# A fused attention and two feed-forward layers on one core: the stores of the weight and x2 jobs move from the SyncE queue to the ScalarE queue

## The chip, the core and the metric

The kernel runs on one core of one Trainium2 chip. The metric is the device time of one execution in microseconds (us), taken outside the profiler as the median of several runs. A profile is one more execution, recorded instruction by instruction.

## What is computed

Attention over short windows, then two feed-forward layers, in float32. The reference, cut to what matters:

```python
for c in range(S // 32):                      # B, H, S, D = 4, 8, 768, 64
    k_full = cat(mem_k, k[:, :, 32*c-16 : 32*c+40])   # 8 + 56 keys, clipped at the ends
    a = softmax(q_c @ k_full.T / 8)
    out_c = a @ cat(mem_v, v[same window])
x = out.reshape(3072, 512)
h = x @ w_in            # 512 x 2048
x = softplus(h) @ w_out # 2048 x 512, first layer
h = x @ w_in2
y = (h - tanh(h)) @ w_out2   # second layer
```

## The kernel before, in words

Each float32 operand of a matmul is split into a high part and a low part, and three products (high·high, high·low, low·high) make one product. The splits cost ScalarE a copy and VectorE a subtraction each, and both are needed for weights (`w`), inputs (`x`) and activations (`gh`, `gl`).

The 3072 tokens are worked in this order. Up to about 427 us, the first layer goes over tiles of 512 tokens in the plain way (`ff_h`, `ff_y1`), while the attention units that are still to come run between its matmuls. From there, four phases of 1024 tokens (the last third of layer 1, then all of layer 2) use a Strassen-like scheme with 7 products in place of 8: `h_phase` (about 76 us) and then `y_phase` (about 76 us) for each. In `h_phase` a product takes TensorE 1.36 us and goes to one of eight accumulator banks. ScalarE copies the partial results out (`kept`, line 701), VectorE adds (`sum`, line 706), and ScalarE applies softplus or tanh (lines 427 and 737).

The scheme needs weights and inputs that are sums of blocks. *Jobs* prepare them beside the main work: `job_w1` and `job_w` (weights of layers 1 and 2) and `job_x` (inputs of a phase). A job reads a tile, forms the sums on VectorE, splits them into high and low parts in buffers of the pool `o` (four buffers; `job_x` also uses `gh` and `gl`), and stores those to scratch memory in DRAM: `wid` (w_in), `wod` (w_out), `x2d` (inputs). `Ring.add` (line 684) and `x2_load` (line 645) load them again later. `job_w` begins with the load of a raw weight tile (line 477, named `w<-in_w2i` or `w<-in_w2o`), and `LEAD` = 3 ticks later it uses it on ScalarE (line 481). Lines 463 and 467 split into `o`; line 600 does the high part in `job_x`.

The order is fixed by hand. A *tick* (function `tick`) is one step of the schedule: it first issues what was deferred to this tick, then the instructions of the main chain, and then one step of each active job. Every engine executes its instructions in the order in which the program emits them. The DMAs are all issued by SyncE (SP in the profile), which does nothing else, so a transfer that has to wait for its data holds up every transfer behind it:

```python
lo = opool.tile([P, *shape], F32R, name="o")
nc.vector.tensor_tensor(out=lo, in0=src, in1=hi.bitcast(F32), op=ALU.subtract)
defer(put, lo, dst(1))          # line 468: issued at the start of the next tick
```

The compiled program tells of a DMA's landing by one of eight semaphores, DMAHW0 to DMAHW7. All DMAs of the program take them in turn, in program order, whichever engine issues them. Before a DMA is issued, its engine waits until the DMA that had the same semaphore before it (eight places earlier) has landed, unless the engine is known to have waited for that already.

Of the kernel before, what the change touches and what calls it, by code (L numbers as in the profile page):

```python
# [8 lines left out]
F32 = mybir.dt.float32  # L9
# [90 lines left out]
def attention_ffn_ffn(  # L100
# [10 lines left out]
    nc = tc.nc  # L111
# [105 lines left out]
    def run(steps):  # L217
        for _ in steps:
            pass
# [4 lines left out]
    def x_tile(j):  # L224
        if j not in xt:
            xt[j] = xpool.tile([P, KT, 2, N], F32R, name=f"x{j % 2}")
        return xt[j]
# [3 lines left out]
    def qk_load(u):  # L231
        t = apool.tile([P, NPAIR * (P + NCH * KEYS)], F32, name="qk")
        nc.sync.dma_start(out=t, in_=qk[u])
        q = t[:, : NPAIR * P].rearrange("p (a t) -> p a t", a=NPAIR)
        k = t[:, NPAIR * P :].rearrange("p (c a k) -> p c a k", c=NCH, a=NPAIR)
        att[u] = dict(q=q, k=k)
# [18 lines left out]
    def v_load(u, v=None):  # L255
        v = apool.tile([P, NCH, NPAIR, D], F32, name="v") if v is None else v
        nc.sync.dma_start(out=v.rearrange("p c a d -> p (c a d)"), in_=vv[u])
        att[u]["v"] = v
# [76 lines left out]
    def t_mm(u, ps):  # L335
        a = att[u]
        for p in range(NPAIR):
            nc.tensor.transpose(  # L338
                ps[:, p * P : (p + 1) * P], a["sm"][:, p * P : (p + 1) * P], ident
            )  # L340
        a["t"] = ps

    def t_out(u):
        a = att[u]
        if u < UB:
            pT = early[:, UB + u].rearrange("p (a t) -> p a t", a=NPAIR)
        else:
            pT = apool.tile([P, NPAIR, P], F32, name="pT", bufs=1)
        a["pT"] = pT
        nc.scalar.copy(out=pT.rearrange("p a t -> p (a t)"), in_=a.pop("t"))  # L350
# [110 lines left out]
    def split_to(src, dst, shape):  # L461
        hi = opool.tile([P, *shape], F32R, name="o")
        nc.scalar.copy(out=hi, in_=src)
        yield
        put(hi, dst(0))
        lo = opool.tile([P, *shape], F32R, name="o")
        nc.vector.tensor_tensor(out=lo, in0=src, in1=hi.bitcast(F32), op=ALU.subtract)
        defer(put, lo, dst(1))

    def put(t, places):  # L470
        for at, n, place in places:
            nc.sync.dma_start(out=place, in_=t[:, at : at + n].bitcast(F32))

    def job_w(kind, p, slot):
        src = w2i if kind == "i" else w2o
# [107 lines left out]
    def job_x(b, e, slot, spare):  # L583
        raw = wpool.tile([P, 2, 2, N], F32, name=f"w{slot}")
        nc.sync.dma_start(out=raw, in_=y1d[b][e])
        for _ in range(LEAD):
            yield
        b11, b21, b12, b22 = raw[:, 0, 0], raw[:, 0, 1], raw[:, 1, 0], raw[:, 1, 1]
        o = {}

        def high(q, src):
            if spare and q in (2, 5, 7):
                h, l = (gpool.tile([P, N], F32R, name=n) for n in ("gh", "gl"))
                stores = [(x2d[b][q - 1][:, e, s], t) for s, t in enumerate((h, l))]
            else:
                t = opool.tile([P, 2, N], F32R, name="o")
                h, l = t[:, 0], t[:, 1]
                stores = [(x2d[b][q - 1][:, e], t)]
            o[q] = h, l, src, stores
            nc.scalar.copy(out=h, in_=src)  # L600

        def low(q):
            h, l, src, stores = o.pop(q)
            minus(l, src, h.bitcast(F32))
            for place, t in stores:
                defer(nc.sync.dma_start, place, t.bitcast(F32))

        high(1, b11)
        high(2, b21)
        yield  # L610
        low(1)
        low(2)
        minus(b12, b12, b11)
        high(3, b22)
        yield
        low(3)
        minus(b22, b22, b12)
        high(5, b12)
        yield
        low(5)  # L620
        minus(b11, b22, b11)
        high(6, b22)
        yield
        low(6)
        minus(b21, b21, b22)
        high(7, b11)
        yield
        low(7)
        high(4, b21)
        yield  # L630
        low(4)
# [77 lines left out]
    def minus(out, x, y):  # L709
        nc.vector.tensor_tensor(out=out, in0=x, in1=y, op=ALU.subtract)  # L710
# [126 lines left out]
        if f == NF - 1:  # L837
            out1(j)

    plan, now, active, late = {}, [0], [], []  # L840
    W2 = [("i", p) for p in range(NP)] + [("o", p) for p in range(NP)]
    for t, kind, p in JOBS_W1:
        plan.setdefault(t, []).append(lambda x=(kind, p): job_w1(*x))
# [7 lines left out]
    place = [0, 0]  # L851
    soft = {}

    def defer(f, *args, more=0):
        late.append((now[0] + more, f, args))

    def tick(chain=iter(())):
        k = now[0]
        now[0] += 1
        calls, late[:] = [x for x in late if x[0] <= k], [x for x in late if x[0] > k]  # L860
        for _, f, args in calls:
            f(*args)
        if k in starts:
            place[:] = starts[k], k
        i, r = place[0], k - place[1]
        u = ATT_ORDER[i] if i < len(ATT_ORDER) else None
        before = ATT_ORDER[i - 1] if 0 < i <= len(ATT_ORDER) else None
        if u is not None:
            if r == 1:
                if i + 2 < len(ATT_ORDER):  # L870
                    qk_load(ATT_ORDER[i + 2])
                if 0 < i < len(ATT_ORDER) - 1:
                    v_load(ATT_ORDER[i + 1])
                next(soft[u])
            elif r == 2:
                run(soft.pop(u))
        if r == 1 and before in VIA_DRAM:
            run(soft.pop(("x", before)))
        if r == 0 and before is not None:
            v_mm(before, ps_a)  # L880
        if r == 0 and u is not None:
            s_mm(u, ps_a)
        if r == 4 and u is not None:
            t_mm(u, ps_a[:, 0, :])
        next(chain, None)
        if r == 4 and u is not None:
            t_out(u)
        next(chain, None)
        if r == 0 and before is not None:
            soft["x", before] = (x_out if before // UB < PLAIN else x_out_whole)(before)  # L890
            next(soft["x", before])
        if r == 0 and u is not None:
            soft[u] = softmax(u)
            next(soft[u])
        if r == 0 and before is not None:
            next(soft["x", before], None)
        run(chain)
        active.extend(job() for job in plan.get(k, ()))
        for job in active[:]:
            if next(job, active) is active:  # L900
                active.remove(job)

    with tc.manual_schedule(engines={mybir.EngineType.PE}):
# [10 lines left out]
        if True:  # L914
# [31 lines left out]
            for token in OPENING.split():  # L946
# [7 lines left out]
                elif op == "Z":  # L954
                    for _ in range(i):
                        nc.tensor.matmul(  # L956
                            out=ps_h[1], lhsT=zeros[:, :P], rhs=zeros, start=True, stop=True
# [23 lines left out]
                else:  # L981
                    if op == "y":
                        going["w", i] = split_w(raws[str(i)], i)
                    elif op[0] == "y":
                        k = "io".index(op[1])
# [8 lines left out]
        for j in range(1, PLAIN):  # L994
            x = x_tile(j)
# [38 lines left out]
            y_phase(b, prep, prepared)  # L1034
        while posts:
            step()
        for _, f, args in late:
            f(*args)
        fixed.close()

# [63 lines left out]
```

## Time and profile before

| | before |
|---|---|
| median of 3 runs | 1055.62 us (1055.35 to 1057.42) |
| profiled execution, own time | 1056.95 us |
| its span in the trace | 1055.1 us |
| TensorE (PE) busy | 1037.2 us, 98% of the span |
| VectorE (DVE) busy | 768.8 us, 73% |
| ScalarE (ACT) busy | 615.3 us, 58% |
| DMAs issued by SyncE | 532 |

The span is what the trace covers, and the profiled execution took 1.85 us more than that. Busy time of an engine does not count issuing a DMA or waiting. A row of a timeline reads: start, duration, engine, source line, operation, what it writes and reads, and in brackets how long the engine stood idle before it and who ended that. SPq, ACTq and so on are the engines' sequencers. Issues that wait show the waiting in the duration when several are merged into one row (x2, x4).

### The profile page before, as it was taken

To read this page: it belongs to the slowest core of one execution; us is meant where nothing else is said; L and a number is where in the kernel's file an instruction comes from. 1 tells how busy PE (TensorE), PEld (TensorE's weight loads), DVE (VectorE), ACT (ScalarE), POOL (GpSimd) and SP (SyncE) were. 2 spreads that over 40 slices of the span, in tenths; PEclk is the share of its full clock that TensorE was granted. 3 is DMA by queue.
4 is the path that set the end of the run, shared out by engine and by line. 5 is a ranking of instruction groups with operands and counts; after the bars stand their busy time and mean duration, and the time that the engine had idled before them with its cause. 6 is when DMAs were issued, how large, how long until landed. Compare 5 with 4: busy or idle time off the path is not lost.

```text
span 1055.1 us, 18599 instructions
## 1 busy us (share of the span) xinstructions
PE 1037.2 (98%) x7320; PEld 848.7 (80%) x7322; DVE 768.8 (73%) x1215; ACT 615.3 (58%) x966; POOL 7.4 (1%) x14
## 2 busy tenths in 40 slices
PE   7999999999999999998999999999999999999998
PEld 5787888888888888787878878888888888888886
DVE  6998477777976785766587696777477877446876
ACT  6997455666666675665565555545455554444553
POOL 1000000000000000000000000000000000000000
PEclk8999999999999999999999999999999999999999
DMA  9999886888998986999999999888898888655661
GB/s 375 408 327 337 277 293 230 285 281 324 319 351 272 338 291 223 343 399 385 368 349 350 339 353 361 324 297 321 305 352 300 315 321 309 225 168 209 242 203 60
DMA packets 112663, 319.99 MB, mean 303 GB/s; under 512 B 8512, under 2 KB 67392, under 8 KB 94144
## 3 DMA queue, kind: packets, MB, share of 16 engines
q1 hardware_dynamic: 112576, 318.80, 84.3%
q8 instruction: 58, 0.95, 0.4%
q14 instruction: 29, 0.24, 0.1%
HBM read 220.73 MB, written 98.04 MB: 302 GB/s over the span
## 4 chain that ended last, share of the span: by engine, by line
PE 88%; DMA 5%; DVE 4%; ACT 2%; issue 1%; SPq 0%; ACTq 0%; DVEq 0%
PE ps_y L404 43%; PE ps_h L404 28%; PE ps_b L404 12%; PE ps_a L367 2%; DMA w<-in_w2o 2%; PE ps_a L286 1%; DMA ring<-wid 1%; PE ps_a L338 1%; DVE w L710 1%; DMA wod<-o 1%; DVE gl L710 1%; DMA x<-wid 1%; DMA qk<-in_qk 0%; PE ps_yy L367 0%; PE ps_h L956 0%
## 5 line engine op out<-in xcount | busy, mean ns | idle before, releaser
L773 ACT CAST gh<-w 128x512 fp32r<-128x512 f32 x224 | 139.3, 623 | 137.2 <-DVE gl L710 106.0
L710 DVE TENSOR_TENSOR gl<-w,gh 128x512 fp32r<-128x512 f32 x239 | 164.4, 690 | 65.0 <-ACT gh L773 59.1
L404 PE MATMUL ps_h<-x,w 128*128 128x512 f32 x756 | 182.2, 391 | 0.1
L404 PE MATMUL ps_y<-gh,w 128*128 128x512 f32 x512 | 171.9, 398 | 0.0
L404 PEld LDWEIGHTS ps_h<-x,w 128*128 128x128 f32 x756 | 141.1, 188 | 30.2 <-issue 0.6
L404 PE MATMUL ps_y<-w,x 128*128 128x512 f32 x504 | 119.5, 389 | 0.0
L404 PE MATMUL ps_y<-gh,x 128*128 128x512 f32 x384 | 119.2, 389 | 0.0
L404 PEld LDWEIGHTS ps_y<-gh,w 128*128 128x128 f32 x512 | 96.1, 188 | 21.1
L404 PEld LDWEIGHTS ps_y<-w,x 128*128 128x128 f32 x504 | 94.6, 188 | 19.7
L404 PE MATMUL ps_y<-gl,w 128*128 128x512 f32 x256 | 99.7, 390 | 0.0
L404 PEld LDWEIGHTS ps_y<-gh,x 128*128 128x128 f32 x384 | 72.1, 188 | 15.0
L737 ACT ACTIVATE tanh<-sum 128x512 f32<-128x512 f32 x72 | 45.4, 632 | 57.3 <-DVE sum L706 57.2
L404 PE MATMUL ps_y<-gl,x 128*128 128x512 f32 x192 | 74.9, 390 | 0.0
L404 PE MATMUL ps_b<-gh,x 128*128 128x512 f32 x192 | 74.7, 389 | 0.0
L404 PE MATMUL ps_h<-gh,x 128*128 128x512 f32 x192 | 74.7, 389 | 0.0
L444 DVE TENSOR_TENSOR gl<-t,gh 128x512 fp32r<-128x512 f32 x64 | 45.5, 713 | 37.6 <-ACT gh L439 37.6
L427 ACT ACTIVATE t<-ps_h 128x512 f32<-128x512 f32 x64 | 38.3, 598 | 57.4 <-PE ps_h L404 53.8
L404 PE MATMUL ps_h<-w,x 128*128 128x512 f32 x252 | 65.2, 395 | 0.7 <-DMA x<-wid 0.7
L404 PE MATMUL ps_b<-w,x 128*128 128x512 f32 x252 | 64.2, 390 | 0.9 <-DVE sum L706 0.9
L706 DVE TENSOR_TENSOR sum<-ps_y,kept 128x512 f32<-128x512 f32 x48 | 32.6, 688 | 41.3 <-PE ps_y L404 35.7
L710 DVE TENSOR_TENSOR w<-w 128x512 f32<-128x512 f32 x88 | 60.4, 688 | 1.8 <-ACT w L427 0.8
L404 PEld LDWEIGHTS ps_h<-w,x 128*128 128x128 f32 x252 | 48.1, 191 | 11.3 <-DMA x<-wid 1.1
(161 smaller groups left out, 1661.4 us busy)
## 6 DMA issues: line engine op xcount, KB each, us to landing
x<-wod SPq DMA_DIRECT2D x48, 1024.0 KB, 5.2
x<-wid SPq DMA_DIRECT2D x24, 1024.0 KB, 7.1
w<-x2d SPq DMA_DIRECT2D x21, 1024.0 KB, 7.5
x<-wid SPq DMA_DIRECT2D x24, 768.0 KB, 6.5
wod<-o SPq DMA_DIRECT2D x32, 512.0 KB, 7.7
wid<-o SPq DMA_DIRECT2D x32, 512.0 KB, 5.6
qk<-in_qk SPq DMA_DIRECT2D x21, 768.0 KB, 6.6
x2d<-o SPq DMA_DIRECT2D x27, 512.0 KB, 8.3
```

What stands on the lines that cost most here:

```text
L286: nc.tensor.matmul(out=ps[cc, j, KEYS * p : KEYS * (p + 1)], lhsT=a["q"][r, p, cc], rhs=a["k"][r, c, p, :], start=True, stop=True,)
L338: nc.tensor.transpose(ps[:, p * P : (p + 1) * P], a["sm"][:, p * P : (p + 1) * P], ident)
L367: nc.tensor.matmul(out=ps[h : h + 64, p % 2, 2 * P + t0 : 2 * P + t0 + CHUNK], lhsT=v, rhs=pT, start=True, stop=True,)
L404: nc.tensor.matmul(out=ps, lhsT=a, rhs=b, start=first and i == 0, stop=last and i == 2, skip_group_check=on,)
L427: nc.scalar.activation(out=out, in_=x, func=AF.Softplus)
L444: eng.tensor_tensor(out=gl, in0=t, in1=gh.bitcast(F32), op=ALU.subtract)
L706: nc.vector.tensor_tensor(out=h, in0=ps, in1=t, op=ALU.add)
L710: nc.vector.tensor_tensor(out=out, in0=x, in1=y, op=ALU.subtract)
L737: nc.scalar.activation(out=t, in_=h, func=AF.Tanh)
L773: nc.scalar.copy(out=gh, in_=src)
```

## The change

Two kinds of store, `put` (line 472: all stores of `wid` and `wod` by the jobs) and the stores of `x2d` in `job_x`, are issued by ScalarE in place of SyncE. In the profile before, the former have line 472 and the latter line 862 (where deferred calls run). The store of a high part stays where the job's step stands. The store of a low part, and those of `x2d`, are put into a new list `after`, which the next tick empties behind the instructions of the main chain, where `defer` would have issued them at the tick's start.

```diff
@@ split_to, put
-        defer(put, lo, dst(1))
+        after.append((now[0], put, (lo, dst(1))))
 
     def put(t, places):
         for at, n, place in places:
-            nc.sync.dma_start(out=place, in_=t[:, at : at + n].bitcast(F32))
+            nc.scalar.dma_start(out=place, in_=t[:, at : at + n].bitcast(F32))
@@ job_x, low
             for place, t in stores:
-                defer(nc.sync.dma_start, place, t.bitcast(F32))
+                after.append((now[0], nc.scalar.dma_start, (place, t.bitcast(F32))))
@@ tick, behind run(chain)
         run(chain)
+        calls, after[:] = [x for x in after if x[0] <= k], [x for x in after if x[0] > k]
+        for _, f, args in calls:
+            f(*args)
         active.extend(job() for job in plan.get(k, ()))
@@ at the end
-        for _, f, args in late:
+        for _, f, args in late + after:
             f(*args)
```

Of 532 DMAs, 185 move: 64 of `wod`, 64 of `wid`, 57 of `x2d`. The order of all compute instructions on every engine stays as it was. In the changed file the `x2d` stores bear line 900.

The first place is the SyncE queue at the end of the plain part, where the second input job stores its seven parts (`x2d`) and the ring's first tiles (`x1`, from `wid11` and `wid10`) are loaded. In square brackets stand the semaphores that a DMA waits for: DMAHW0 to 7 for landings, the others for engines. Before:

```order
L684 DMA ring_4862<-wid10_128 128x2048 [waits DMAHW1_49]
L862 DMA x2d05_97<-o_4829 128x1024 [waits DMAHW2_49,DVE_49]
L862 DMA x2d06_98<-o_4848 128x1024 [waits DMAHW3_49,DVE_49,Activation_49]
L862 DMA x2d07_99<-o_4885 128x1024 [waits DMAHW4_49,DVE_49]
L862 DMA x2d04_96<-o_4905 128x1024 [waits DMAHW5_49,DVE_49,Activation_49]
L684 DMA x1_2871<-wid11_129 128x2048 [waits DMAHW6_49,PE_49]
L684 DMA x1_2871<-wid10_128 128x1536 [waits DMAHW7_49,PE_49]
```

With the change:

```order
L684 DMA ring_4862<-wid10_128 128x2048 [waits DMAHW6_49,DMAHW2_49,DMAHW1_49]
L684 DMA x1_2871<-wid11_129 128x2048 [waits DMAHW3_49,PE_49]
L684 DMA x1_2871<-wid10_128 128x1536 [waits DMAHW5_49,PE_49]
L477 DMA w15_4969<-in_w2o 128x2048 [waits DMAHW7_49,DVE_49,Activation_49]
```

The four stores that stood between the ring's loads, and that wait for VectorE, have left this queue.

The second place is the SyncE queue some 50 us later, in the first `h_phase`, around the load of the raw weight tile `w15_5312`. Before:

```order
L684 DMA x1_2871<-wid16_134 128x2048 [waits DMAHW5_49,PE_49]
L862 DMA x2d03_95<-o_5258 128x1024 [waits DMAHW6_49,DVE_49]
L477 DMA w15_5312<-in_w2o 128x2048 [waits DMAHW7_49]
L862 DMA x2d05_97<-gh_5283 128x512 [waits DMAHW0_49,Activation_49]
L862 DMA x2d05_97<-gl_5284 128x512 [waits DMAHW1_49,DVE_49]
L862 DMA x2d06_98<-o_5309 128x1024 [waits DMAHW2_49,DVE_49]
L862 DMA x2d07_99<-gh_5336 128x512 [waits DMAHW3_49,Activation_49]
L862 DMA x2d07_99<-gl_5337 128x512 [waits DMAHW4_49,DVE_49]
L684 DMA x0_5012<-wid17_135 128x2048 [waits DMAHW5_49,PE_49]
L684 DMA x0_5012<-wid16_134 128x1536 [waits DMAHW6_49,PE_49]
```

With the change:

```order
L684 DMA x1_2871<-wid15_133 128x1536 [waits DMAHW3_49,DMAHW2_49,PE_49]
L684 DMA x1_2871<-wid16_134 128x2048 [waits DMAHW5_49,PE_49]
L477 DMA w15_5312<-in_w2o 128x2048 [waits DMAHW6_49,DVE_49]
L684 DMA x0_5012<-wid17_135 128x2048 [waits DMAHW3_49,PE_49]
L684 DMA x0_5012<-wid16_134 128x1536 [waits DMAHW4_49,PE_49]
```

The loads now follow each other, and the load of `w15_5312` waits for the semaphore DMAHW6 (last used by the load of `x0_5012<-wid15`) where it waited for DMAHW7 (last used by `ring<-wid14`).

The third place is ScalarE at the same point of the program, from the copies `kept` of two banks to the use of `w15_5312` (L481) and beyond. Before:

```order
L701 COPY kept_5369<-ps_b0_4860 128x512 [waits PE_49]
L701 COPY kept_5377<-ps_h0_81 128x512 [waits PE_49]
L463 CAST o_5382<-w14_5212 128x768 [waits DMAHW1_49,DVE_49]
L481 ACTIVATE w15_5312<-w15_5312,low_bias_138 128x1024 [waits DMAHW7_49]
L701 COPY kept_5392<-ps_b1_4861 128x512 [waits PE_49,Activation_49]
L701 COPY kept_5401<-ps_h1_82 128x512 [waits PE_49,Activation_49]
L427 ACTIVATE w12_5320<-sum_5419 128x512 [waits DVE_49]
```

With the change:

```order
L900 DMA x2d07_99<-gh_5336 128x512 [waits DMAHW5_49,Activation_49]
L900 DMA x2d07_99<-gl_5337 128x512 [waits DMAHW6_49,DVE_49]
L463 CAST o_5382<-w14_5212 128x768 [waits DVE_49]
L481 ACTIVATE w15_5312<-w15_5312,low_bias_138 128x1024
L701 COPY kept_5392<-ps_b1_4861 128x512 [waits PE_49]
L701 COPY kept_5401<-ps_h1_82 128x512 [waits PE_49]
L900 DMA x2d04_96<-o_5359 128x1024 [waits DMAHW7_49,DVE_49]
L472 DMA wod2_127<-o_5382 128x2x256 [waits DMAHW0_49,Activation_49]
L472 DMA wod2_127<-o_5382 128x256 [waits DMAHW1_49]
L427 ACTIVATE w12_5320<-sum_5419 128x512 [waits DVE_49]
L472 DMA wod2_127<-o_5406 128x2x256 [waits DMAHW2_49]
L472 DMA wod2_127<-o_5406 128x256 [waits DMAHW4_49]
```

ScalarE has two stores more ahead of these copies and five more behind them. The store `x2d07<-gl` waits for DMAHW6, the landing of the load of `w15_5312` itself, and it stands ahead of the CAST and of `kept_5392`. The last row's store waits for DMAHW4, the landing of the load `x0_5012<-wid16`.

## Rows read from the trace of the kernel before

**Rows 1.** Stretches: length; busy us (instructions) by engine; TensorE clock; DMA share; GB/s.

```profile
130.00:430.00 300.00, 299.72 (x3191) 246.12 (x3190) 227.57 (x398) 194.36 (x256) 0.00 (x0) 1.00 0.84 290
430.00:500.00 70.00, 66.27 (x284) 54.04 (x283) 45.49 (x68) 42.63 (x67) 0.00 (x0) 0.98 1.02 391
500.00:587.00 87.00, 86.47 (x380) 70.64 (x379) 66.76 (x104) 48.27 (x78) 0.00 (x0) 1.00 0.97 356
587.00:663.00 76.00, 74.83 (x329) 61.10 (x328) 54.63 (x85) 42.81 (x73) 0.00 (x0) 1.00 0.98 351
```

**Rows 2.** TensorE's waits: who waited for whom, us in total, times, longest.

```profile
PE ps_b L404 <- ACT kept L701: 3.0, 1, 3.0
PE ps_b L404 <- DVE sum L706: 0.9, 1, 0.9
PE ps_h L404 <- DMA x<-wid: 0.7, 1, 0.7
```

**Rows 3.** Timeline of SyncE's DMA issues, 414 to 436 us.

```profile
415.83 11.33 SPq L862 DMA_DIRECT2D x2d<-o  x4
427.25 1.21 SPq L684 DMA_DIRECT2D x<-wid  x2
```

**Rows 4.** The chain of work that ended last, 410 to 530 us: start, us, what.

```profile
427.25 7.00 DMA x<-wid
...
463.18 10.14 DMA ring<-wid
...
473.34 12.84 DMA w<-in_w2o
```

**Rows 5.** Timeline of ScalarE, 478 to 489 us.

```profile
479.99 0.88 ACT L463 CAST o<-w 128x768 fp32r<-128x768 f32 x1
486.20 1.19 ACT L481 ACTIVATE w<-w,low_bias 128x1024 uint32<-128x1024 uint32 x1 [5.34 <-DMA w<-in_w2o]
487.30 0.57 ACT L701 COPY kept<-ps_b 128x512 f32<-128x512 f32 x1
```

**Rows 6.** Timeline of TensorE, 484 to 493 us.

```profile
487.92 2.17 PE L404 MATMUL ps_b<-w,ring 128*128 128x512 f32 x6 [3.01 <-ACT kept L701]
489.88 2.66 PE L404 MATMUL ps_h<-w,x 128*128 128x512 f32 x6
```

**Rows 7.** The stretch behind that wait (columns as in group 1).

```profile
488.90:492.20 3.30, 3.30 (x9) 2.54 (x9) 1.65 (x3) 2.91 (x5) 0.00 (x0) 0.50 1.01 347
```

**Rows 8.** Timeline of SyncE's DMA issues, 469 to 488 us.

```profile
471.76 0.42 SPq L862 DMA_DIRECT2D x2d<-o  x1
473.34 0.33 SPq L477 DMA_DIRECT2D w<-in_w2o  x1
...
482.57 1.91 SPq L684 DMA_DIRECT2D x<-wid  x2
```

**Rows 9.** DMAs in 464 to 492 us: queue, packets, MB, share of 16 engines.

```profile
q1 hardware_dynamic: 3129, 11.24, 102.6%
```

**Rows 10.** DMAs issued in 483.8 to 484.4 us: KB, us to landing.

```profile
x<-wid SPq DMA_DIRECT2D x1, 768.0 KB, 11.4
```

**Rows 11.** The moved stores by line and tile: issue ns min/median/max, first and last start.

```profile
L472 SPq DMA_DIRECT2D wod<-o x64: 319/404/1570, 134.9 to 616.2; - x64
L472 SPq DMA_DIRECT2D wid<-o x64: 359/378/2235, 147.4 to 378.5; - x64
L862 SPq DMA_DIRECT2D x2d<-o x27: 319/320/1393, 408.6 to 808.8; - x27
L862 SPq DMA_DIRECT2D x2d<-gh x15: 319/436/1067, 467.7 to 804.9; - x15
L862 SPq DMA_DIRECT2D x2d<-gl x15: 319/436/1313, 468.2 to 807.6; - x15
```

**Rows 12.** ScalarE's waits, 130 to 430 us.

```profile
ACT t L427 <- PE ps_h L404: 49.3, 26, 4.3
```

**Rows 13.** Timeline of ScalarE, 603 to 620 us.

```profile
611.82 0.62 ACT L600 CAST o<-w 128x512 fp32r<-128x512 f32 x1 [2.52 <-DMA wod<-o]
```

More of the change, by code (lines that the diff above doesn't have):

```diff
@@ L838, in run_y @@
             out1(j)
-    plan, now, active, late = {}, [0], [], []
+    plan, now, active, late, after = {}, [0], [], [], []
     W2 = [("i", p) for p in range(NP)] + [("o", p) for p in range(NP)]
```

## Prediction

> **What bounds the kernel now.** I read the stretches first, for TensorE. From 130 us on it is busy nearly all the time: it stands idle 0.28 us of 300 up to 430 us, 3.73 us of 70 up to 500, 0.53 of 87 and 1.17 of 76 after that [rows 1]. That is 5.7 us in all, and a change that moves stores can give back no more than this, and what the clock adds to it. TensorE's waits name the larger pieces: one wait of 3.0 us for a ScalarE copy `kept`, one of 0.9 us for a VectorE sum, one of 0.7 us for a load `x<-wid` [rows 2].
>
> The reader is to see how two of them come out of the SyncE queue. At 415.83 us SyncE begins four input stores and is done with them 11.33 us later, because each waits for its VectorE subtraction; only then, at 427.25, do the ring's loads go out [rows 3]. Such a load takes 7.00 us in the chain [rows 4], and its tail is the 0.7 us wait. Some 50 us on, a raw weight load is issued at 473.34 [rows 8], just when an unrelated `ring<-wid` load has landed (463.18 + 10.14 = 473.32), and lands 12.84 us later, at 486.18 [rows 4]. ScalarE needs it and stands idle 5.34 us; the copy `kept` is queued behind it [rows 5], and TensorE waits 3.01 us for that copy [rows 6]. So ScalarE could have been 5.34 - 3.01 = 2.33 us late here at no cost. That slack is the measure for all that follows. Behind the wait the clock is granted at half (1.2 of 2.4 GHz) for some 3.3 us [rows 7]: the next two groups of six matmuls end at 489.88 + 2.66 = 492.54, 4.6 us after 487.92 [rows 6], where two take 2.7 at full clock (329 matmuls in 74.83 us [rows 1]): 1.9 us lost. The DMA engines are full in this stretch (102.6% of 16 engines [rows 9]), so landings come late because work is queued, whoever issues it.
>
> **The change part by part.** Durations are from the profiled execution, 1056.95 us (span 1055.1), which lies 1.3 us above the median of the runs, 1055.62. I sum differences, and put them on the median at the end.
>
> *Issues moved.* By the medians, 64 x 0.404 + 64 x 0.378 + 27 x 0.320 + 30 x 0.436 = 72 us of issuing move to ScalarE [rows 11]. In the plain part the cover is ScalarE's waiting for TensorE, 49.3 us in 26 waits of up to 4.3 us [rows 12], and 300 - 194 = 106 us idle [rows 1]; some 100 of the 185 issues fall there by the timeline's count, 40 us. In the second `h_phase` stretch ScalarE is idle 76 - 43 = 33 us, and 20 issues need some 9 [rows 1]. I cost issuing at 0 there. Without the cover it would show where several issues stand between two copies: four in a row are 1.6 us, still under 2.33. In the `y_phase`, where ScalarE makes one `gh` for each 1.36 us of TensorE, ten issues of 0.4 us meet 87 - 48 = 39 us idle [rows 1]: 0. Upper ends: 1.5 us for the plain part, 1 for the `y_phase`, 2 for the later `h_phase`s.
>
> *The ring's first loads.* The four stores leave the queue, and with them up to 11.33 us of waiting [rows 3], of which 0.7 is enough; the loads then wait for TensorE alone. The 0.7 us wait goes: **-0.7** (ends -0.7 and 0).
>
> *The wait of 3.01 us.* Here two things happen. The weight load no longer waits for the ring load's landing and can go out in place of the store of 471.76, 1.6 us earlier. In a full queue only what is ahead counts: that store's 512 KB at 401 GB/s (11.24 MB in 28 us [rows 9]) is 1.3 us. So it would land at 484.9. Against it, ScalarE now has two stores and the CAST ahead of its use. The second of these stores waits for the landing of this very weight load, since it takes the same semaphore. The CAST (0.88 us [rows 5]), which was done during the waiting, now comes after it, with an issue of 0.32: +1.2. If the transfers keep the order of issue, the balance is 1.2 - 1.3 = -0.1. If instead stores from ScalarE's queue get their share at once, while the loads of SyncE's queue are backed up, then the two further stores issued in the meantime (`x2d05`, `x2d06`, 1.3 us each) pass the weight load, and the store of 471.76 is ahead as before: 1.2 + 2.6 = +3.8. No row has two busy queues, one carried 3129 packets of this stretch [rows 9]. I take one store passing more than the order allows: **+2.5** (ends -0.1 and +3.8). The half-speed stretch stays.
>
> The Trainium skill, "DMA: Bandwidth & Descriptors", section "Queues, rings and completion order", says that each DMA engine goes round the queue rows it has work for, packet by packet, and that SyncE and ScalarE each own a row. By that rule stores would pass backed-up loads, and this term would be its upper end, +3.8; no run here shows it yet.
>
> *The next blocking store.* A few instructions on, a store on ScalarE waits for the load issued about 483.9, which takes 11.4 us and lands at 495.2 [rows 10]. SyncE absorbed that; ScalarE was at this place at about 490, a copy and an activation after its `kept` of 487.30 [rows 5]. Late by the term above and by the issues, it comes at 493 to 494 and waits 1 to 2 us, under the slack if the slack is whole again: **+0.6** (ends 0 and 5.2 - 2.33 = +2.9). What is late next is softplus of that tile, then the next `kept`.
>
> *Buffers.* At 611.82 ScalarE waits 2.52 us for a buffer `o` whose store has not landed [rows 13]; the TensorE wait of 0.9 us follows some 8 us on [rows 2]. From its own queue that store goes ahead of the loads, but ScalarE gets some eight issues (3 us) on the way. I take half: **-0.5** (ends -0.9 and +1).
>
> Sum: -0.7 + 2.5 + 0.6 - 0.5 = +1.9 us, so 1055.62 + 1.9 = **1057.5 us**.
>
> **The rivals.** *Loads come sooner and ScalarE is not held up (faster).* The loads leave early everywhere, no store on ScalarE waits over 2.33 us. The 3.01 us wait shrinks by 1.3, the half-speed stretch goes (1.9), and the 0.7 and 0.9 us waits go, with some 0.3 of the rest: -5.1, 1050.5 us. For it speaks that 5.34 us of ScalarE's waiting was for one late load; against it that the store on the same semaphore keeps ScalarE from doing the CAST meanwhile. At the very most all 5.7 us and 1.9 go: 1048.
>
> *ScalarE stands still for old landings (slower).* In a stretch with landings of 10 to 13 us, a store that waits for the DMA eight places back stops everything behind it on ScalarE: `kept`, then TensorE. It decides from 2.33 us of waiting on. With both upper ends, 3.8 + 2.9, less the 0.7: +6.0, 1061.6 us; with the ends of the issuing terms too, some 1066.
>
> *Nothing arrives.* Only the 0.7 us goes and the rest is hidden: 1055 us. The Trainium skill, same page, section "Issuing engines are not separate DMA queues", says that all these transfers run on the same 16 DMA engines and that issuing from several only saves issue time. By that rule there is no gain here beyond the freed SyncE queue, and this rival would hold unless ScalarE pays.
>
> **How the numbers follow.** Forecast 0.37 (its own range 1055.5 to 1060), faster rival 0.28, slower rival 0.25, nothing 0.10. A measurement of this kernel tells 0.2%, 2.1 us. The forecast lies on both sides of +0.2%: 0.24 same, 0.13 slower. The faster rival gives 0.28 and 0.01 comes from the forecast's low end. So faster 0.29, same 0.34, slower 0.37. The range takes in the faster rival's middle and most of the slower one: 1050 to 1064 leaves out the ends of both, some 2 in 10.
>
> **What would show it.** The 0.7 us wait for `x<-wid` near 434 us should be gone. Near 485 us TensorE should still wait for `kept`, for 4 to 6 us, with ScalarE stopped in front of an `x2d` store, and the weight load landing not earlier than 486. ScalarE's busy time should be the same, with about 185 issues among its instructions. Plain part and layer 2 should be as before. I am wrong if that wait has shrunk to under 2 us and the clock stays whole (the faster rival), or if waits for `kept`, `gl` or `sum` appear in other `h_phase`s and in the `y_phase`s (the slower one).

## The result and the profile after

The changed kernel takes 1064.77 us (median; 1063.59 to 1066.63), the kernel before 1055.70 us on the same chip: 9.1 us more, a ratio of 1.0075 with a 95% interval of 1.0058 to 1.0092. It is slower, clear of the noise. The median lies 0.8 us above the range of 1050 to 1064 us that was given; the ratio, put on the 1055.62 us from which the prediction counted, gives 1063.5 us, just inside its upper end. The profiled execution of after took 1065.05 us (span 1062.8), 8.1 us more than that of before.

The stretches of the changed kernel, with the columns of [rows 1]:

```profile
130.00:430.00 300.00, 296.35 (x3175) 243.13 (x3174) 222.31 (x389) 192.30 (x253) 0.00 (x0) 1.00 0.84 287
430.00:500.00 70.00, 67.56 (x295) 54.62 (x293) 45.57 (x68) 40.64 (x64) 0.00 (x0) 1.00 1.03 396
500.00:587.00 87.00, 82.11 (x349) 67.10 (x350) 64.99 (x100) 48.59 (x79) 0.00 (x0) 0.96 0.91 332
587.00:663.00 76.00, 74.17 (x325) 60.47 (x323) 55.05 (x86) 41.12 (x68) 0.00 (x0) 1.00 0.96 343
```

Two stretches got much worse: the plain part, where TensorE now stands idle 3.65 us in place of 0.28, and the `y_phase` behind 500 us (4.89 us for 0.53, and a clock of 0.96). The stretch from 430 to 500 us, where the prediction expected the loss, got better by 1.3 us. In the four stretches together TensorE's idle time grew from 5.7 to 12.8 us.

TensorE's waits in the changed kernel from 130 us on (who waited for whom: us in total, times, longest):

```profile
PE ps_y L404 <- ACT kept L701: 4.9, 1, 4.9
PE ps_b L404 <- ACT kept L701: 4.1, 5, 1.6
PE ps_a L338 <- DVE sm L333: 3.4, 1, 3.4
PE ps_b L404 <- DVE gl L710: 0.5, 1, 0.5
```

Against [rows 2], the waits for the load `x<-wid` and for the VectorE sum are gone, the 3.0 us for `kept` have become 4.1 in five pieces, and two waits are new (4.9 and 3.4 us). The timeline of TensorE says where the larger ones are, and the first of three small ones near 622, 629 and 663 us:

```profile
361.37 0.63 PE L338 MATMUL ps_a<-ident,sm 128*128 128x128 f32 x4 [3.37 <-DVE sm L333]
...
479.56 1.66 PE L404 MATMUL ps_b<-w,x 128*128 128x512 f32 x6 [1.61 <-ACT kept L701]
...
488.34 1.65 PE L404 MATMUL ps_b<-w,ring 128*128 128x512 f32 x6 [0.32 <-ACT kept L701]
...
504.42 7.76 PE L404 MATMUL ps_y<-w,x 128*128 128x512 f32 x22 [4.87 <-ACT kept L701]
...
623.17 1.65 PE L404 MATMUL ps_b<-w,x 128*128 128x512 f32 x6 [0.68 <-ACT kept L701]
```

The row at 504.42 also shows the clock: 22 matmuls take 7.76 us, where 24 took 5.60 us just ahead of the wait, so some 2.6 us are lost (estimate from these two figures); in 502 to 510 us the granted clock is 0.57, that is 1.2 GHz for most of it. TensorE had stood idle 4.87 us before it fell.

**The plain part.** Timeline of ScalarE in the changed kernel (ACTq rows are its DMA issues):

```profile
343.07 1.06 ACTq L472 DMA_DIRECT2D wid<-o  x2
...
351.80 1.10 ACT L463 CAST o<-w 128x1024 fp32r<-128x1024 f32 x1 [4.30 <-DMA wid<-o]
```

The same for VectorE, the engine that makes `sm`:

```profile
355.51 1.22 DVE L467 TENSOR_TENSOR o<-w,o 128x1024 fp32r<-128x1024 f32 x1 [4.44 <-DMA wid<-o]
...
360.53 0.69 DVE L333 TENSOR_TENSOR sm<-sm,st 128x512 f32<-128x512 f32 x1
```

And the chain of work that ended last (start, us, what), which names the landings behind all three large waits:

```profile
343.48 11.91 DMA wid<-o
...
464.46 13.45 DMA wod<-o
...
489.70 13.21 DMA wod<-o
```

Near 358 us the order is: a weight store lands 11.91 us after its issue, at 355.39; the next tile's subtraction on VectorE needs that buffer `o` and has waited 4.44 us; `sm` stands behind it on VectorE; TensorE waits 3.37 us for `sm`. In the kernel before the same cast and subtraction waited 2.28 and 0.65 us, and for `y1d` stores issued ahead of these weight stores:

```profile
351.41 1.14 ACT L463 CAST o<-w 128x1024 fp32r<-128x1024 f32 x1 [2.28 <-DMA y1d<-o]
...
353.35 1.23 DVE L467 TENSOR_TENSOR o<-w,o 128x1024 fp32r<-128x1024 f32 x1 [0.65 <-DMA y1d<-o]
```

**The full stretch.** DMAs of the changed kernel in 455 to 495 us: queues (packets, MB, share of 16 engines), then issues (KB each, median us to landing). q1 is SyncE's queue, q10 ScalarE's.

```profile
q1 hardware_dynamic: 1569, 10.40, 62.9%
q10 hardware_dynamic: 3481, 5.61, 39.6%
...
x<-wid SPq DMA_DIRECT2D x3, 1024.0 KB, 7.1
w<-in_w2o SPq DMA_DIRECT2D x2, 1024.0 KB, 8.9
...
wod<-o ACTq DMA_DIRECT2D x2, 512.0 KB, 13.2
wod<-o ACTq DMA_DIRECT2D x3, 256.0 KB, 13.7
```

In the kernel before, the same stretch on one queue:

```profile
x<-wid SPq DMA_DIRECT2D x3, 1024.0 KB, 10.6
w<-in_w2o SPq DMA_DIRECT2D x2, 1024.0 KB, 11.3
...
wod<-o SPq DMA_DIRECT2D x2, 512.0 KB, 10.1
wod<-o SPq DMA_DIRECT2D x2, 256.0 KB, 9.7
```

With one queue these transfers landed after about 10 us, loads and stores alike. With two, the loads shown land 2.4 to 3.5 us sooner and the weight stores 3 to 4 us later, though the loads carry more bytes. The loads gain on the stores; the prediction had feared the reverse. Near 500 us ScalarE pays for it (its timeline):

```profile
491.12 5.51 ACTq L472 DMA_DIRECT2D wod<-o  x2
496.67 1.12 ACT L487 ACTIVATE w<-w 128x1024 f32<-128x1024 f32 x1 [5.02 <-DMA x<-wid]
...
503.00 0.88 ACT L463 CAST o<-w 128x768 fp32r<-128x768 f32 x1 [1.67 <-DMA wod<-o]
503.79 0.58 ACT L701 COPY kept<-ps_y 128x512 f32<-128x512 f32 x1
```

First the second of two stores waits about 5 us for the landing of a load (the DMA eight places back, on whose semaphore it is counted). Then the CAST needs the buffer `o` whose store went out at 489.70 and lands at 502.90, and only behind the CAST comes the `kept` that TensorE waits for. In the kernel before the same CAST waited 1.66 us:

```profile
497.59 0.88 ACT L463 CAST o<-w 128x768 fp32r<-128x768 f32 x1 [1.66 <-DMA wod<-o]
```

One of the small waits in layer 2 has another source. Near 622 us four issues stand in a row on ScalarE, from 619.08 to 621.97, of 0.34 to 1.11 us each; a CAST of `gh`, with the `kept` behind it, has to wait until they are done:

```profile
622.01 0.62 ACT L600 CAST gh<-w 128x512 fp32r<-128x512 f32 x1 [2.35 <-issue]
```

Over 130 to 663 us, ScalarE's waits for stores to release `o` or `gh` grew from 14.8 to 28.2 us, those for loads into `w` fell from 15.7 to 5.4, and 7.3 us of waits in front of an issue that itself waits for a landing are new (the last row below is the larger part). The largest of the changed kernel (columns as for TensorE's waits):

```profile
ACT o L463 <- DMA wid<-o: 9.2, 4, 4.3
ACT o L600 <- DMA wod<-o: 7.9, 4, 2.8
ACT o L600 <- DMA x2d<-o: 6.8, 2, 4.1
ACT w L487 <- DMA x<-wid: 5.0, 1, 5.0
```

So in this stretch the loads gained and the buffers paid.

### The profile page after: what moved, and what is told of

Its sections match the earlier page's. It is cut to its first block, busy times and chain, and to the rows that moved or that the text cites. A ratio compares the mean times of both kernels' runs of the same rounds, so it can differ in the third digit from the quotient of the medians.

```text
span 1062.8 us, 18521 instructions
## 1 busy us (share of the span) xinstructions
PE 1035.6 (97%) x7320; PEld 846.2 (80%) x7322; DVE 768.9 (72%) x1215; ACT 615.4 (58%) x966; POOL 7.9 (1%) x14
## 4 chain that ended last, share of the span: by engine, by line
PE 81%; DMA 7%; DVE 6%; ACT 4%; issue 1%; ACTq 1%; DVEq 0%
PE ps_y L404 41%; PE ps_h L404 25%; PE ps_b L404 12%; DMA wod<-o 3%; DMA x2d<-o 2%; PE ps_a L367 2%; PE ps_a L286 1%; DMA wid<-o 1%; DVE w L710 1%; DMA x2d<-gl 1%; PE ps_a L338 1%; DVE gl L710 1%; DMA qk<-in_qk 0%; ACT o L173 0%; ACT t L427 0%
## 5 line engine op out<-in xcount | busy, mean ns | idle before, releaser
L404 PE MATMUL ps_y<-w,x 128*128 128x512 f32 x504 | 122.2, 395 | 4.9 <-ACT kept L701 4.9
L404 PEld LDWEIGHTS ps_b<-w,x 128*128 128x128 f32 x252 | 46.9, 188 | 15.5 <-ACT kept L701 6.0
```

What stands on the lines that cost most here:

```text
L404: nc.tensor.matmul(out=ps, lhsT=a, rhs=b, start=first and i == 0, stop=last and i == 2, skip_group_check=on,)
```

## The experiments

Each run was timed in turn with the kernel before on one chip, and the ratio to it is given with its 95% interval. The changed kernel has 1.0075, which is 7.9 us; the 9.1 us in the expectations are the difference of the medians. Each run's own profiled execution gives the waits. In the built programs an edit of this section also moves which DMA shares a semaphore with which, so a single wait can change for more than one reason.

**Which stores?** Only `x2d` moved:

```diff
-        after.append((now[0], put, (lo, dst(1))))
+        defer(put, lo, dst(1))
...
-            nc.scalar.dma_start(out=place, in_=t[:, at : at + n].bitcast(F32))
+            nc.sync.dma_start(out=place, in_=t[:, at : at + n].bitcast(F32))
```

> Only the x2d stores go to ScalarE; the weight stores stay on SyncE as in the kernel before. Theory (ScalarE stands still where a weight store waits for an old landing, and buffers o come free later because those stores are issued later): the TensorE gaps near 358 us (3.4) and near 500 us (4.9, and the half clock behind it) belong to weight stores and are gone, the 0.7 us wait near 434 us stays gone; 1054 to 1057 us. Rival A (the issuing itself costs ScalarE time, 72 us for 185 issues): x2d is 57 issues and some 22 us of the 72, so about 0.3 of the 9.1 us loss stays: 1058.5. Rival B (the slower half of the loss is that two queues slow each other's transfers): x2d stores lie in the fullest stretch, so most of the loss stays, 1061 or more.

Measured: 1061.99 us, 1.0051 [1.0032, 1.0070]. The two gaps of the theory are gone, yet 5.4 us of loss are left. The time is rival B's, but not its mechanism: in 430 to 510 us the 512 KB `x2d` stores landed after 7.8 us where they took 10.7 before. The trace has a larger wait in a place that no theory named: 5.1 us for `kept` near 484 us, where the kernel before waits 3.0. (The profiled execution, 1058.77 us, was the fastest of this run, so its trace shows less than the whole loss.) ScalarE waits for the raw weight load, and that load left late. SyncE's waits, 460 to 490 us:

```profile
SPq L477 <- DMA x2d<-gl: 9.4, 1, 9.4
```

SyncE stood 9.4 us in front of the load until an `x2d` store of ScalarE landed. The two share no data, only a semaphore: eight semaphores are dealt out in turn to all DMAs of the program, so the queues can stop each other through them. The reverse half, only the weight stores moved:

```diff
-                after.append((now[0], nc.scalar.dma_start, (place, t.bitcast(F32))))
+                defer(nc.sync.dma_start, place, t.bitcast(F32))
```

> Only the weight stores go to ScalarE; the x2d stores stay on SyncE as in the kernel before. Theory: the gaps near 358 and 500 us stay, the 0.7 us wait near 434 us is back, and the loss is 7 us or more: 1062 to 1066. Rival A (cost of issuing): 128 issues and some 50 us of the 72, so 0.7 of the 9.1 us: 1062. It differs from the theory by a loss spread over many small waits. Rival B (two queues): 1057 to 1059, since the stretch at 430 to 500 us then has few stores on the second queue.

Measured: 1074.00 us, 1.0164 [1.0142, 1.0186], worse than the whole change and 8 us above the theory's range. TensorE's waits:

```profile
PE ps_b L404 <- ACT kept L701: 8.0, 3, 3.3
PE ps_a L338 <- DVE sm L333: 3.5, 1, 3.5
PE ps_y L404 <- ACT kept L701: 3.1, 1, 3.1
```

The parts don't add up (5.4 + 17.3 for 7.9, by the ratios), so no sum by issues can hold, and rival A is out in that form. Behind three of the four waits for `kept` ScalarE waited 5.4 to 7.7 us for a buffer `o` (a `wod` store), behind the fourth 4.5 us for the raw weight load.

**The later place or the queue?**

```diff
-            nc.scalar.dma_start(out=place, in_=t[:, at : at + n].bitcast(F32))
+            nc.sync.dma_start(out=place, in_=t[:, at : at + n].bitcast(F32))
...
-                after.append((now[0], nc.scalar.dma_start, (place, t.bitcast(F32))))
+                after.append((now[0], nc.sync.dma_start, (place, t.bitcast(F32))))
```

> The stores are issued at the same later place in the program as in the changed kernel, but all by SyncE. Theory: no compute engine waits for the landing eight places back, so the 5.0 us stop of ScalarE near 492 us and its gap of 4.9 us on TensorE are gone; what later issue does to buffers o stays, so a part of the 3.4 us near 358 us may stay; 1055 to 1060. Rival A (cost of issuing on ScalarE): 1055.7. Rival C (it is the later place alone that costs, whatever queue): 1063 to 1066.

Measured: 1056.07 us, 0.9997 [0.9983, 1.0012]. Issuing behind the tick's main chain in place of ahead of it costs nothing. The whole loss comes with issuing from ScalarE. What it is there that costs, this run doesn't say: 1056.07 is in the theory's range and is rival A's number too. The 0.7 us wait near 434 us stays away here too, and the 3.0 us wait is there as before (2.9). The same with `nc.gpsimd` in both lines:

> The moved stores are issued by GpSimd, which has nothing else to do in these stretches, at the place of the changed kernel. Theory: the engine that stands still is then one for which nobody waits, so the stop of 5.0 us near 492 us is gone; buffers o still come free late: 1055 to 1060. Rival A (cost of issuing on ScalarE): 1055.7. Rival B (transfers from a second queue land later): 1062 to 1066, with the same landings of 12 to 13 us.

Measured: 1106.87 us, 1.0477 [1.0454, 1.0500]. That is above every range that was given, and it doesn't tell the theories apart: an issue takes GpSimd 0.74 us (median), and TensorE's waits lie in new places, above all in the plain part:

```profile
PE ps_a L338 <- DVE sm L333: 19.9, 4, 5.8
```

**The plain part alone.**

```diff
+        if now[0] < 88:
+            defer(put, lo, dst(1), nc.sync)
+        else:
             after.append((now[0], put, (lo, dst(1))))
...
-            nc.scalar.dma_start(
+            (q or (nc.sync if now[0] < 88 else nc.scalar)).dma_start(
```

> The changed kernel, but the weight stores of the plain part (some 95 issues, up to about 400 us) go to SyncE as before; the stores behind it stay on ScalarE. Theory (a store that ScalarE issues late lands late and holds one of the four buffers o): the TensorE gap of 3.4 us near 358 us is gone and nothing else changes, 1060 to 1062. Rival (the issues cost ScalarE time everywhere): half of the issues are gone, so half of the 9.1 us: 1060, but then with the gap near 358 us only partly smaller and with less idle time of ScalarE in the changed kernel elsewhere in the plain part. If the plain part's stores keep the later part in step by chance, 1064 or more.

Measured: 1061.46 us, 1.0043 [1.0024, 1.0062]: 3.4 us less than the changed kernel by the ratios, as much as the gap near 358 us, which is gone (the two intervals leave that difference uncertain by some 2.7 us). The waits for `kept` stay at 7.9 us in all, for 9.0 in the changed kernel, in part at other places.

**The pair that stops ScalarE near 492 us**, put on SyncE:

```diff
-            nc.scalar.dma_start(
+            (nc.sync if now[0] == 117 else nc.scalar).dma_start(
```

> The changed kernel with one pair of weight stores put on SyncE, the two of which the second keeps ScalarE waiting 5.0 us near 492 us for the landing eight places back; place in the program and semaphores stay. Theory 1 (that wait is what delays the copy kept): the TensorE gap of 4.9 us near 500 us and the half clock behind it go, some 7 us: 1057 to 1059. Theory 2 (the delay comes from the buffer o, whose earlier store lands at 502.9 whatever ScalarE does meanwhile): the gap stays at 3 us or more, 1062 to 1066.

Measured: 1063.74 us, 1.0072 [1.0050, 1.0094], not to be told from the changed kernel. That time is theory 2's, but the trace is neither's:

```profile
493.78 1.66 PE L404 MATMUL ps_b<-w,ring 128*128 128x512 f32 x6 [1.71 <-ACT kept L701]
...
506.48 5.74 PE L404 MATMUL ps_y<-w,x 128*128 128x512 f32 x24 [1.52 <-ACT kept L701]
```

The 4.9 us have become 1.5, 1.4 us have come up earlier, and ScalarE now stands 5.7 us in front of an `x2d` store and two other weight stores. The expectation that place and semaphores stay did not hold: in the built program the pair stands ahead of those stores and the semaphores are dealt out anew, and one more tile takes a buffer used two tiles earlier (table below). So it shows that a stop can move along the queue, and not how much this one was worth.

**A buffer more behind the plain part**, for the first tile of each weight store:

```diff
-        hi = opool.tile([P, *shape], F32R, name="o")
+        if now[0] > 90:
+            hi = tpool.tile([P, *shape], F32R, name="c2", bufs=1)
+        else:
+            hi = opool.tile([P, *shape], F32R, name="o")
```

> The changed kernel, but behind the plain part (from about 430 us) the first of the two tiles of each weight store lies in a buffer of its own that is free by then, so that four buffers o and a fifth serve the stores. Theory (late landings hold the four buffers o): the gaps near 478 us (1.6) and 500 us (4.9, and the half clock, some 2 us) shrink by more than half, and the waits of 0.7 to 0.8 us near 622, 629 and 663 us too; the 3.4 us near 358 us stay; 1055 to 1058. Rival (ScalarE stands still for landings eight places back): the 5.0 us stop near 492 us stays and TensorE waits there as before; 1062 or more.

Measured: 1085.36 us, 1.0261 [1.0228, 1.0294]. The edit was a bad one: first tiles now wait for the store of the one before, 23.1 us in 6 waits (`ACT c L466 <- DMA wod<-c`). It says only how dear a buffer is that is held until its store has landed. The same edit with the plain part's stores on SyncE:

> Both edits together: the plain part's weight stores on SyncE as before, and the fifth buffer behind it. Theory (buffers): all larger gaps of the changed kernel are gone and its gain (the 0.7 us wait near 434 us and most of the 3.0 us wait near 485 us, with the half clock behind it) is left: 1050 to 1054, faster than both kernels. Rival (waiting for landings on ScalarE): 1058 or more.

Measured: 1078.67 us, 1.0200 [1.0174, 1.0225], with the same fault.

**Who gets which buffer.** In the built programs I then counted, for each of the 182 tiles `o`, how many tiles earlier its buffer had been used (the first four have none), and set beside it TensorE's wait for `sm` from 130 us on:

```
kernel               2   3    4    5   6 tiles earlier   wait for sm, longest (us)
before               0   7  165    5   1                 none
changed              2  11  153    9   3                 3.4
only x2d             0   9  161    7   1                 none
only weight stores   3  14  146   10   5                 3.5
later, on SyncE      0   7  165    5   1                 0.2
plain part SyncE     0   9  161    7   1                 none
pair on SyncE        3  11  150   11   3                 4.3
window on SyncE      3   9  154    9   3                 4.5
on GpSimd            5   8  150   12   3                 5.8
```

The pool doesn't hand out buffers in plain turn, and in these programs its choice changes with the engine that issues a store: `after` on SyncE deals as before does. With ScalarE, the two tiles near 351 to 356 us take the buffers used two tiles earlier, whose stores went out at 340 to 343 us, although two older ones, last used for `y1d` stores, were next in turn (the kernel before takes those). The wait for `sm` is long exactly where a 2 is ("window on SyncE" is the last run of this section). The test is a fixed turn:

```diff
+    def o_tile(shape, dtype):
+        i = turn[0] % 4
+        turn[0] += 1
+        return opool.tile(shape, dtype, name=f"o{i}", bufs=1)
...
-        hi = opool.tile([P, *shape], F32R, name="o")
+        hi = o_tile([P, *shape], F32R)
```

> The changed kernel, but the four buffers o are given out in fixed turn, so that each tile takes the buffer used four tiles earlier. In the built program of the change two tiles of the plain part take the buffer used two tiles earlier, which in the kernel before none does. Theory (the 3.4 us gap near 358 us comes from these two tiles, which wait for stores issued 10 us before, and not from ScalarE's issuing): that gap is gone, the waits at 478 to 504 us, where the turn is the same as before, stay; 1060 to 1062. Rival (late stores from ScalarE's queue make the gap): it stays at 2 us or more, 1064.

Measured: 1062.89 us, 1.0053 [1.0035, 1.0070]. The gap near 358 us is gone, the rest stands:

```profile
PE ps_y L411 <- ACT kept L708: 5.3, 1, 5.3
PE ps_b L411 <- ACT kept L708: 3.4, 4, 1.4
```

The same turn in the kernel before:

> The kernel before with the same fixed turn: the control. Theory: its buffers are dealt almost in turn already (7 of 182 tiles take one used three tiles earlier), so nothing moves: 1054.5 to 1057. Rival (the turn itself gains or loses something in every stretch): outside of that, and then the same amount is to be taken off the run with the change.

Measured: 1057.33 us, 1.0014 [1.0005, 1.0022]: the turn itself costs 1.5 us by the ratio, and the median lies 0.3 us over what was expected. Against it the fixed turn leaves 4.1 us of the change's loss (1.0053 less 1.0014), so the dealing of buffers made up some 3.8 of 7.9. The intervals leave this uncertain by some 2.7 us; the gap itself, 3.37 us in the trace and gone here, is the firmer figure.

**Five buffers in turn**, behind the plain part:

```diff
+        i = turn[0] % (5 if now[0] > 90 else 4)
+        turn[0] += 1
+        if i == 4:
+            return tpool.tile(shape, dtype, name="c2", bufs=1)
```

> The changed kernel with the fixed turn, and behind the plain part a turn of five buffers in place of four. Theory (behind the plain part the loss is stores from ScalarE's queue that land late, 13 us in the worst place, and hold the buffers o): with five, the waits for kept near 478 and 500 us and those of 0.7 to 0.8 us near 622, 629 and 663 us shrink by more than half; 1054 to 1057. Rival (ScalarE stands still for the landing eight places back): they stay, 1060 to 1062.

Measured: 1060.08 us, 1.0038 [1.0026, 1.0050]; by the time the rival's number (and not clear of the 1.0053 with four buffers), by the waits in between:

```profile
PE ps_b L413 <- ACT kept L710: 2.6, 2, 1.5
PE ps_y L413 <- DVE sum L715: 2.2, 1, 2.2
...
PE ps_y L413 <- ACT kept L710: 0.6, 1, 0.6
```

The 5.3 us wait near 500 us is 0.6, and the CAST there no longer waits for its buffer: so it was the buffer that held this `kept` up. But 2.2 us of it have come back right behind, and again a buffer is the reason: VectorE waits for a store that went out at 490.00 and landed 11.90 us later, and the `sum` stands behind that.

```profile
502.10 0.96 DVE L476 TENSOR_TENSOR o<-w,o 128x768 fp32r<-128x768 f32 x1 [2.40 <-DMA wod<-o]
```

ScalarE still stops in front of an issue for the landing of a load, now for 2.6 us, and the raw weight load's wait is 1.5 us again.

**The full stretch alone**, 430 to 510 us, with its stores as before:

```diff
+        if 94 <= now[0] < 126:
+            defer(put, lo, dst(1), nc.sync)
+        else:
             after.append((now[0], put, (lo, dst(1))))
```

(and the same condition for the queue and for `x2d`).

> The changed kernel with all stores issued between about 430 and 510 us as before, by SyncE; the plain part and what comes behind stay on ScalarE. Theory (losses are local to the stretch): the gaps near 478 and 500 us and the half clock are gone and the 3.0 us wait near 485 us is back, the gap near 358 us stays: about 4 us less than the changed kernel, 1059 to 1062. Rival (a store on one queue also holds up the issues of the other through the shared semaphores, so that a mixture is no better than the whole): 1064 or more.

Measured: 1068.91 us, 1.0106 [1.0090, 1.0123]: the rival's case, the mixture is worse than the whole. TensorE's waits:

```profile
PE ps_b L404 <- ACT kept L707: 5.3, 2, 3.1
PE ps_a L338 <- DVE sm L333: 4.5, 1, 4.5
PE ps_h L404 <- DMA x<-wid: 1.5, 1, 1.5
PE ps_b L404 <- ACT gh L779: 1.3, 1, 1.3
```

The gaps at 478 and 500 us are gone and the 3.1 us wait is back, as expected, but the gap in the plain part grew and 2.1 us appeared near 627 us, in a stretch whose issues had not been edited. Near 627 us ScalarE first waited 2.73 us for a buffer (a `wod` store) and then had four issues in a row (624.08 to 627.31) ahead of that `kept`; in the plain part the CAST waited 5.49 us for its buffer, for 4.30 in the changed kernel. Why these were longer here stays open. So the losses aren't local to the stretch; but what the trace names in these two places is buffers and issuing, so the rival's reason, the shared semaphores, is not shown by its number.

## Where the prediction held and where it failed

The forecast of 1057.5 us and its mechanism did not come. The time lies at the upper edge of the range only because the range had been drawn wide for the slower rival (a chance of 0.25, at 1061.6 us). That rival's mechanism, ScalarE waiting for old landings, came in part: its stop in front of an issue is there, but its largest term, +3.8 at the raw weight load, is not, and the buffers and the plain part, which make up most of the loss, stand in neither sum. So the edge of the range was met by luck. Both signs of being wrong came too: the wait near 485 us fell under 2 us, and waits for `kept` appeared in other phases. By its own steps:

- **Issues moved: 0, upper end +1.5 for the plain part.** As a price of issuing this nearly held: the four issues in a row near 622 us took 2.9 us, not the 1.6 that was counted, and cost TensorE 0.7. But "Plain part and layer 2 should be as before" failed: +3.4 us near 358. The step that failed is that the plain part was priced only by issuing. It did not ask whether the buffers would be dealt out in the same order; that could have been read from the built program without a run.
- **The ring's first loads: -0.7.** Right; the wait near 434 us is gone in every kernel whose `x2d` stores leave the front of SyncE's queue, and there again where they stay (0.6 and 1.5 us).
- **The wait of 3.01 us: +2.5.** Wrong in sign. It is 1.61 + 0.32 us now, so -1.1, and the half-speed stretch of 1.9 us, which was to stay, has gone from here. The step that failed is "I take one store passing more than the order allows". The weight load was not held back by stores: it went out at 475.26, later than before, and landed after 10.1 us in place of 12.84 [rows 4], at 485.4. ScalarE did stop in front of the store on its semaphore, as foreseen, but only until then. Part of the small wait is owed to the other losses: TensorE, held up near 358 and 478 us, was ready here at 488.0 in place of 484.9. With the plain part's stores on SyncE, and with five buffers, 0.95 and 1.5 us of it are back.
- **The next blocking store: +0.6, ends 0 and +2.9.** The right place and the right wait (a store on ScalarE that waits 5.0 us for a load landing at 496.3), mis-sized: 4.9 us of TensorE and some 2.6 us of half clock behind them. The term counted one wait against the slack of 2.33 us. It left out the buffer behind it, whose store landed 13.2 us after issue.
- **Buffers: -0.5, ends -0.9 and +1.** The wait read at 611 us went as expected (2.52 us is 1.46 now, and TensorE's 0.9 us are gone), but three waits for `kept` of 0.7 to 0.8 us near 622, 629 and 663 us came, 2.2 us in all. What was mis-sized is the price of the issues on the way, and that a later `x2d` store holds a buffer too (2.69 us of ScalarE's waiting ahead of the `kept` near 629 us).
- **Nothing arrives.** The same stores at the same place of the program differ by some 8 us between SyncE and ScalarE, so this rival is out. The Trainium skill, "DMA: Bandwidth & Descriptors", section "Issuing engines are not separate DMA queues", says that all transfers run on the same 16 DMA engines and that starting them from several issuing engines only saves the time of issuing. The first half agrees with the trace: 391 GB/s in 430 to 500 us before, 396 after. The second does not hold here: with two queues loads landed sooner and weight stores later than with one, and ScalarE and the buffers waited for that.

Added up in these terms: plain part +3.4, ring -0.7, weight load -1.1 and -1.9 of half clock, blocking store +4.9 and +2.6 of half clock, buffers and issues in layer 2 -0.9 and +2.2; that is +8.5 us, where the span grew by 7.7. The two that carry it, the plain part and the blocking store with the buffer behind it, had been put at 0 and +0.6.

The wrong turn of the third step came out of one rule read in one direction. The Trainium skill, same page, section "Queues, rings and completion order", says that a DMA engine goes round the queues with work, packet by packet. I drew from it that the stores would pass the loads. In 487 to 503 us SyncE's queue moved 576 packets and 3.67 MB with 55.8% of the engines' time, ScalarE's 1702 packets and 2.33 MB with 45.0%. The time was shared about evenly, the packets as counted here were not. That neither queue stands behind the other's backlog agrees with this trace; who gains by it has to be worked out from what stands in each queue. My reading is that ScalarE's queue held the longer backlog, of smaller packets; no run tests that alone.

The two parts as far as they are shown: the dealing of buffers is some 3.4 to 3.8 us of the loss (two undoings, plain part and fixed turn, and the gap of 3.37 us in the trace). Near 500 us buffers held TensorE up, since a fifth one takes 5.3 us there to 0.6 and 2.2. Open is how much of the rest is stops in front of issues, how much late landing and how much issuing itself, and whether five buffers would gain the same with all stores on SyncE; that was not run. No version here beats the kernel before by more than its uncertainty.

## What to carry to other kernels

Before moving stores to a compute engine's queue, list what each later tile waits for: the buffer it is given, and the DMA on whose semaphore it is counted; both can change with the queue alone. In this full stretch a second queue added no bandwidth (391 GB/s before, 396 after), it re-dealt lateness: loads landed 2.4 to 3.5 us sooner, weight stores 3 to 4 us later, and the loser matters if a small pool of buffers hangs on it. SyncE, on which nothing is computed, could wait at no cost (the run with the later place was level with before).

## What was not expected of the hardware and its program

- In 487 to 503 us two queues shared the DMA engines' time nearly evenly (55.8% to 45.0%) with packets of 6.4 and 1.4 KB on average, and a load issued at 493 us (`ring<-wid`, 6.7 us) landed before stores issued 3 to 5 us earlier (13.2 to 13.4 us).
- Waits on semaphores dealt out in turn couple the queues: SyncE stood 9.4 us in front of a load for a store of ScalarE.
- An issue of a weight store took GpSimd 0.74 us where ScalarE took 0.37 to 0.38 (medians). Issues in a row on ScalarE took longer: near 620 us four took 2.9 us.
